# Three-operation float64 conversion through PSUM, and Newton operations one step later, in the first mixture layer

## The chip, the cores and the metric

The kernel runs on one core of a Trainium2 chip. A core has TensorE (PE in the rows; its weight loads are PEld), VectorE (DVE), ScalarE (ACT), GpSimd (POOL) and SyncE (SP, which issues DMAs). The engines run their own instruction streams in order and wait for one another by semaphores. The metric is device time in microseconds (us), from one launch to its end.

## The reference

Three layers follow one another. The first is attention over 4 batches and 8 heads of 512 local and 32 global positions (2304 tokens after the transpose, 512 features). The second, called the first mixture layer here, is a dense layer with a rational activation:

```
h = x @ w_in                                   # 2304x512 @ 512x2048, w_in is float64
P = a[0] + a[1]*h + a[2]*h*h + a[3]*h*h*h
Q = 1 + |b[0]|*|h| + |b[1]|*h*h
x = ((P / (Q + 1e-6)) @ w_out).astype(float32)  # w_out is float64 too
```

The third is a layer of eight experts, each token sent to one. Only the first mixture layer and the conversion of its weights are changed.

## The kernel before

**Weights.** `w_in` and `w_out` come in as float64, as pairs of 32-bit words (low, high). They are worked on in 16 pieces f of 128 hidden units, each with two halves (`w_in`, `w_out`), so there are 32 half pieces of 128x512 elements. `conv` (L881) turns one half into float32. ScalarE takes the magnitude of the high word (L886). VectorE shifts and masks the high word (L887, L888); after a `yield`, so in a later step of the pipeline, it adds bits of the low word (L890) and multiplies with a test for tiny values (L891). The intermediate `st_x` lies in SBUF. `wsplit` (L906) then splits the float32 into two parts, high (ScalarE, L913) and the rest (POOL, L914), since TensorE multiplies in a short format and three products (high x high, high x low, low x high) stand for one.

**Steps.** The layer is cut into 80 steps n = (group g of four pieces f) x (5 blocks of tokens: 512, 512, 384, 384, 384) x (4 pieces). So a group has 20 steps: 8 of 512 tokens and 12 of 384. Steps 0 to 3 are computed within the tail of the attention; the loop of `moe1` runs from step 4 (PRE). In step n:

- `gemm1(n)` (L933): 12 matmuls of 512 or 384 columns into a PSUM bank `h`.
- `poly` (L939 to L942): ScalarE writes `u`, `v`, `t` from `h`; POOL adds `u` and `v` (this is Q - 1).
- `split` of step n-1 (L970 ScalarE, L971 POOL): the finished quotient `t` into `gh` and `gl`.
- `gemm2(n-3)` (L1005 to L1007): 3 matmuls of 512 columns for each 128 tokens, into PSUM banks `o` that gather over the four pieces of a group.
- `poly2` (L947, L948 on VectorE): the polynomial in `t`.
- `inv` (L954, L955 on ScalarE): a first estimate of 1/Q by logarithm and exponential, written over `h`.
- `evac`: where a block's fourth piece is done, VectorE and ScalarE take its `o` banks out (L1013, L1017, L1020; POOL adds for some, L1018).
- `wstep`: one half of a conversion, in most steps.
- `inv2` (L960 to L962 on VectorE): a Newton step on the estimate and the product, `t` being the result.

**What sets the order.** Instructions are issued in the order in which the Python code names them, and each engine keeps it. PSUM has eight banks: four for `o` and two each of the kinds `s` and `t`. From step 4 to step 59 (NSHARE = 60) `hbank` gives `h` all four of `s` and `t` in turn; from step 60 on only the two of `s`, and `t` serves other tiles. `u`, `v` and `t` in SBUF have two buffers each. In the attention a hand-written list of letters (`A_ORDER`) sets the order of each unit's parts; its letter C is one `wstep`.

Of the kernel before, what the change touches and what calls it, by code (L numbers as in the profile page):

```python
# [7 lines left out]
F32 = mybir.dt.float32  # L8
F32R = mybir.dt.float32r
I32 = mybir.dt.int32  # L10
U32 = mybir.dt.uint32
I64 = mybir.dt.int64
AF = mybir.ActivationFunctionType
ALU = mybir.AluOpType
# [5 lines left out]
P = 128  # L20
B, H, SL, SG, D = 4, 8, 512, 32, 64
# [50 lines left out]
PRE = 4  # L72
BLOCKS = [(0, 512), (512, 512), (1024, 384), (1408, 384), (1792, 384)]

NSHARE = 60
KS = [(g, blk, f) for g, grp in enumerate(GROUPS) for blk in BLOCKS for f in grp]


# [4 lines left out]
class Kernel:  # L83
# [5 lines left out]
    def build(self):  # L89
        tc, nc = self.tc, self.nc  # L90
        with ExitStack() as ctx:
# [4 lines left out]
            with tc.manual_schedule(), ExitStack() as pctx, ExitStack() as xctx:  # L96
                self.consts()
                self.xp = ctx.enter_context(tc.tile_pool(name="xp", bufs=1))
                self.xt_hi, self.xt_lo = ([
                    [self.xtile(x, p, c, [P, n], F32R) for p, n in enumerate((HT, NT - HT))] for c in range(NDC)  # L100
                ] for x in ("hi", "lo"))
                self.wr = [[self.xp.tile([P, 2, 4 * CH], F32R, name="wr00")]]
                stage = xctx.enter_context(tc.tile_pool(name="stage", bufs=1, side="right"))
                self.st_raw = [stage.tile([P, CH], F32, name=f"st_raw{i}") for i in range(2)]
                self.st_m = [stage.tile([P, DM], F32, name=f"st_m{i}") for i in range(4)]
                self.st_x = stage.tile([P, DM], U32, name="st_x")
                self.tail = xctx.enter_context(tc.tile_pool(name="tail", bufs=1, side="right"))
                self.mfree, self.mbusy = list(self.st_m), False
                self.w, self.wm, self.wraw, self.G = {}, [], {}, {}
                self.wconv = self.conv()  # L110
                self.ps = pctx.enter_context(tc.tile_pool(name="ps", bufs=1, space=PSUM))
                self.turn, self.oht, self.stg = {}, None, [None] * NCH
                bctx = pctx.enter_context(ExitStack())
                self.wk = bctx.enter_context(tc.tile_pool(name="wk", bufs=2))
                with ExitStack() as actx:
                    self.attention(actx)
                ring = [self.wr[0][0].rearrange("p a b -> p (a b)"), self.tail.tile([P, 4 * CH], F32R, tag="t", name="wslot")]
                self.slot = [ring[i // 4][:, i % 4 * 4 * DM:(i % 4 + 1) * 4 * DM] for i in range(NWR)]
                self.moe1(bctx, ctx, xctx)
                bctx.close()  # L120
                self.moe2_alloc(ctx)
                self.first_hi(range(4, NCH))
                self.route()
# [392 lines left out]
    def attention(self, ctx):  # L516
# [15 lines left out]
        st = {}  # L532
# [4 lines left out]
        def load(u):  # L537
            b, hp = units[u]
            h0 = 2 * hp
            if hp == 0:  # L540
# [1 line left out]
                nc.sync.dma_start(g[0:SG], io["q_g"][b].rearrange("h s d -> s h d"))  # L542
                nc.sync.dma_start(g[SG:], io["k_g"][b].rearrange("h s d -> s h d"))
                st["g", b] = g
            q = self.wk.tile([P, 4, 2, D], F32, tag="t", name="q")
            k = self.wk.tile([P, 4, 2, D], F32, tag="u", name="k")
            for t, src in ((k, "k_l"), (q, "q_l")):
                for h in range(2):
# [327 lines left out]
        self.wraw[f, half] = st  # L876

    def conv(self):
        nc = self.nc
        for f in range(NFC):  # L880
            for half in range(2):  # L881
                st = self.wraw.pop((f, half))
                lo, hi = st[:, :, 0], st[:, :, 1]
                m, x = self.mfree.pop(0), self.st_x
                self.mbusy = True
                nc.scalar.activation(m, hi.bitcast(F32), AF.Abs)  # L886
                nc.vector.tensor_scalar(x, hi, 0x07FFFFFF, 3, ALU.bitwise_and, ALU.logical_shift_left)  # L887
                nc.vector.scalar_tensor_tensor(x, hi, 0xC0000000, x, ALU.bitwise_and, ALU.bitwise_or)  # L888
                yield
                nc.vector.scalar_tensor_tensor(x, lo, 29, x, ALU.logical_shift_right, ALU.bitwise_or)  # L890
                nc.vector.scalar_tensor_tensor(m, m, 2.0 ** -15, x.bitcast(F32), ALU.is_ge, ALU.mult)  # L891
                self.wm.append((f, half, m))
                self.mbusy = False
                if f + 1 < NFC:
# [22 lines left out]
    def hbank(self, k):  # L917

        i = KS.index(k)
        return "st"[i % 2] if PRE <= i < NSHARE else "s"  # L920

    def gemm1(self, k):
        nc = self.nc
        g, (t0, n), f = k
        wh, wl = self.w[f, 0]
        h = self.bank(self.hbank(k), "h")[:, :n]
        self.G[k] = [h] + [self.wk.tile([P, 512], F32, tag=nm, name=nm)[:, :n] for nm in "tuv"]
        i = 0
        for c in range(NDC):
            cs = slice(c * P, (c + 1) * P)  # L930
# [53 lines left out]
    def moe1(self, ctx, kctx, xctx):  # L984
# [111 lines left out]
        while len(pend) > LAG:  # L1096
            gemm2(pend.pop(0))
        for n in range(PRE, NK):
            if n == NSHARE:
                self.lp = self.bank("t", "lp")  # L1100
            while (ks[n][2], 0) not in self.w or n >= LAG and (ks[n - LAG][2], 1) not in self.w:
                self.wstep(freed if n >= LAG else (-2, -2))
# [5 lines left out]
                parts.append((full[0], logits(full.pop())))  # L1108
            elif fin:
                final(fin.pop(0))  # L1110
            if n > 0:
                self.split(ks[n - 1])
            pend.append(ks[n])
            while len(pend) > LAG:
                gemm2(pend.pop(0))
            for x in now:
                logits2(*x)
            self.poly2(ks[n])
            self.inv(ks[n])
            for d in done:  # L1120
                evac(*d)
            done.clear()
            if side and fin:
                final(fin.pop(0))
            norm()
# [12 lines left out]
            g, blk, f = ks[n - LAG + 1]  # L1138
            if f != GROUPS[g][-1] or blk == BLOCKS[0]:
                self.wstep(freed if n >= LAG else (-2, -2))  # L1140
            self.inv2(ks[n])
        n = NK
        bl = len(BLOCKS) - 1
        final(fin.pop(0))
# [572 lines left out]
```

## Time and profile before

| | us |
|---|---|
| median of three runs (926.14 to 930.65) | 928.39 |
| profiled execution | 927.5 |
| its span in the trace | 925.6 |
| busy PE / DVE / ACT / POOL, whole span | 845.2 / 666.2 / 541.8 / 427.2 |

The attention takes the first 187 us or so, the loop of the first mixture layer stands between 208.7 and about 606 us, and the expert layer follows. Busy shares over the whole span mix these stages. PE's ends are modelled, so that PE counts as busy a little longer than it works: its pace is read from the starts of its matmuls.

### The profile page before, as it was taken

The page shows a single profiled execution, that of the slowest core. Times are in us where ns is not written, and L with a number is a line of the kernel's source. Part 1 is how long each engine was busy: PE and PEld are TensorE (multiplying, and loading weights), DVE is VectorE, ACT ScalarE, POOL GpSimd, SP SyncE. Part 2 cuts the span into 40 slices and gives each one's busy share as a digit, 9 for nine tenths or more (in the row PEclk, how much of TensorE's full clock was granted, in tenths as well). Part 3 has the DMA queues.
Part 4 walks back from the last instruction along what each step waited for, and adds up shares of the span by engine and source line. Part 5 has one row for each costly group of instructions (what it writes and reads, how often), then busy time and mean ns, then how long its engine had stood idle before and what let it go on. Part 6 is the DMA issues. An engine that isn't in the chain of part 4 may idle for free.

```text
span 925.6 us, 17451 instructions
## 1 busy us (share of the span) xinstructions
PE 845.2 (91%) x6015; PEld 714.0 (77%) x6015; DVE 666.2 (72%) x1320; ACT 541.8 (59%) x1180; POOL 427.2 (46%) x381
## 2 busy tenths in 40 slices
PE   7888999879999999999998999977899999999994
PEld 5566777668887878777786888856779889898983
DVE  3786888888998999999998777788726793222620
ACT  5665676557778877777777787764434551113211
POOL 4333333445556676666756543314615781112400
PEclk9997999999999999999999999989899999999998
DMA  7555555201111101111010024236924884111000
GB/s 168 126 135 134 122 129 133 69 23 47 46 46 46 46 24 46 47 46 46 27 44 0 2 77 139 75 131 210 319 80 145 288 313 145 36 35 60 28 25 15
DMA packets 106501, 84.96 MB, mean 92 GB/s; under 512 B 79175, under 2 KB 87367, under 8 KB 106384
## 3 DMA queue, kind: packets, MB, share of 16 engines
q1 hardware_dynamic: 102864, 73.18, 26.8%
q0 software_dynamic: 3520, 10.23, 3.2%
q8 instruction: 72, 1.18, 0.5%
q14 instruction: 45, 0.37, 0.1%
HBM read 74.47 MB, written 10.22 MB: 91 GB/s over the span
## 4 chain that ended last, share of the span: by engine, by line
PE 49%; DVE 32%; issue 7%; ACT 5%; DMA 3%; SPq 2%; POOL 1%; DVEq 0%; ACTq 0%; POOLq 0%
PE d_o L1421 13%; PE d_h L1381 10%; PE h L933 5%; DVE t L948 4%; DVE t L962 4%; DVE h L961 4%; DVE u L960 4%; DVE t L947 4%; PE sb L646 3%; PE d_h L1395 3%; DVE st_x L890 3%; DVE st_x L887 1%; DMA q<-q_l 1%; PE o L1005 1%; PE o L1007 1%
## 5 line engine op out<-in xcount | busy, mean ns | idle before, releaser
L933 PE MATMUL h<-xhi,wr 128*128 128x384 f32 (+1 forms) x480 | 146.2, 365 | 8.0 <-DVE t L962 8.0
L942 POOL TENSOR_TENSOR u<-u,v 128x384 f32<-128x384 f32 (+1 forms) x80 | 92.2, 1153 | 90.3 <-ACT v L940 79.3
L1421 PE MATMUL d_o<-wr,xlo 128*128 (+1 forms) x528 | 127.1, 399 | 7.1 <-DVE wr L1548 3.9
L1421 PEld LDWEIGHTS d_o<-wr,xlo 128*128 128x128 f32 x528 | 99.9, 192 | 29.9 <-issue 6.1
L971 POOL TENSOR_TENSOR gl<-t,gh 128x384 fp32r<-128x384 f32 (+1 forms) x80 | 92.1, 1151 | 63.0 <-issue 36.0
L933 PEld LDWEIGHTS h<-xhi,wr 128*128 128x128 f32 x480 | 90.2, 191 | 18.3 <-DVE t L962 9.0
L1381 PEld LDWEIGHTS d_h<-xlo,wr 128*128 128x128 f32 x768 | 94.6, 195 | 2.9 <-issue 2.3
L1381 PE MATMUL d_h<-xlo,wr 128*128 128x256 f32 x768 | 95.0, 286 | 1.9 <-issue 1.9
L1005 PE MATMUL o<-wr,gh 128*128 128x512 f32 x204 | 82.7, 405 | 8.4 <-DVE x L1020 4.7
L933 PE MATMUL h<-xlo,wr 128*128 128x384 f32 (+1 forms) x240 | 86.8, 362 | 0.0
L1489 ACT ACTIVATE xlo<-d_h 128x512 fp32r<-128x512 f32 x32 | 19.0, 597 | 106.7 <-PE d_h L1381 106.7
L1007 PE MATMUL o<-wr,gl 128*128 128x512 f32 x204 | 80.5, 394 | 0.0
L1006 PE MATMUL o<-wr,gh 128*128 128x512 f32 x204 | 80.4, 394 | 0.0
L970 ACT CAST gh<-t 128x384 fp32r<-128x384 f32 (+1 forms) x80 | 44.9, 561 | 54.3 <-DVE t L962 53.4
L1653 POOL TENSOR_TENSOR wr<-xhi,wr 128x1024 f32 x21 | 61.8, 2956 | 28.1 <-ACT wr L1478 18.5
L1548 DVE TENSOR_TENSOR wr<-xhi,wr 128x1024 f32 x35 | 68.6, 2008 | 3.8 <-issue 3.6
L1639 POOL DMA_INDIRECT out<-xlo,scat x22 | 25.2, 1146 | 89.7 <-DVE xlo L1581 88.4
L1581 DVE TENSOR_SCALAR xlo<-d_o,gate 128x512 f32<-128x512 f32 x22 | 16.4, 748 | 66.2 <-PE d_o L1421 66.2
L960 DVE SCALAR_TENSOR_TENSOR u<-u,h 128x384 f32<-128x384 f32 (+1 forms) x80 | 48.2, 602 | 18.7 <-ACT h L955 13.6
L673 ACT ACTIVATE pr<-pr,nm 128x160 f32<-128x160 f32 x128 | 53.0, 425 | 14.6 <-DVE rs L683 10.5
L687 POOL TENSOR_TENSOR pr<-pr,rs 128x512 f32<-128x512 f32 x32 | 38.8, 1232 | 46.6 <-DVE rs L684 39.6
L941 ACT ACTIVATE t<-h,ab 128x384 f32<-128x384 f32 (+1 forms) x80 | 57.5, 718 | 0.7 <-POOL gl L971 0.7
(288 smaller groups left out, 2069.7 us busy)
## 6 DMA issues: line engine op xcount, KB each, us to landing
xhi<-w SPq DMA_DIRECT2D x64, 512.0 KB, 5.1
st_raw<-w_in SPq DMA_DIRECT2D x16, 512.0 KB, 3.8
st_raw<-w_out SPq DMA_DIRECT2D x16, 512.0 KB, 3.7
x_dram<-x SPq DMA_DIRECT2D x17, 256.0 KB, 2.2
k<-k_l SPq DMA_DIRECT2D x32, 128.0 KB, 3.5
q<-q_l SPq DMA_DIRECT2D x32, 128.0 KB, 3.7
va<-v_l SPq DMA_DIRECT2D x32, 96.0 KB, 2.7
vb<-v_l SPq DMA_DIRECT2D x32, 96.0 KB, 2.7
```

Source lines behind the costliest of these rows:

```text
L933: nc.tensor.matmul(h, w[:, cs], x, start=(i == 0), stop=(i == 3 * NDC - 1))
L941: nc.scalar.activation(t, h, AF.Identity, bias=self.ab[:, 2:3], scale=self.ab[:, 3:4])
L942: nc.gpsimd.tensor_tensor(u, u, v, ALU.add)
L960: nc.vector.scalar_tensor_tensor(u, u, ONE, h, ALU.add, ALU.mult)
L971: nc.gpsimd.tensor_tensor(gl, t, f32(gh), ALU.subtract)
L1005: nc.tensor.matmul(o, gh[:, gs], wh[:, DM:], start=first, stop=False)
L1006: nc.tensor.matmul(o, gh[:, gs], wl[:, DM:], start=False, stop=False)
L1007: nc.tensor.matmul(o, gl[:, gs], wh[:, DM:], start=False, stop=last)
L1381: r = nc.tensor.matmul(o, w(0, par, b, sl), xs[a][:, c], start=(i == 0), stop=(i == len(steps) - 1))
L1421: r = nc.tensor.matmul(po[t], ht[a][h][:, c, t * P:(t + 1) * P], w(1, par, b, sl), start=(h == c == a == b == 0), stop=(h == a == 1 and c ...
L1548: E.tensor_tensor(l_, stg[i], f32(h_), ALU.subtract).then_inc(ld, 1)
L1653: E.tensor_tensor(l_, stg[i], f32(h_), ALU.subtract).then_inc(lp, 1)
```

## The change

1. `conv`: ScalarE copies the high word scaled by 2^-112 into `m` (it took the magnitude before); VectorE's two bit operations read `m` and no longer the raw high word; the last operation writes `m` and the multiplication goes. So VectorE has three operations for a half instead of four, and its first one waits for ScalarE's copy.
2. From step 4 to step 65 the intermediate is a PSUM bank `xb` of the kind `t`, not `st_x`. In the attention it stays `st_x`.
3. `h` then has three banks in turn (`sts`) in place of four, up to step 65 (NSHARE = 66).
4. Up to step 65 `inv2` of step n-1 follows `inv` of step n, and `split` of step n-2 stands where that of n-1 was. `t` has three buffers; `u` and `v` still have two.
5. `evac` of a block's first two tiles stands ahead of `poly2`, the rest behind it and ahead of `inv`.

```diff
-NSHARE = 60
+NSHARE = 66
-            q = self.wk.tile([P, 4, 2, D], F32, tag="t", name="q")
+            q = self.wk.tile([P, 4, 2, D], F32, tag="t", name="q", bufs=3)
...
-                m, x = self.mfree.pop(0), self.st_x
+                m, x = self.mfree.pop(0), self.st_x if self.xb is None else self.xb
-                nc.scalar.activation(m, hi.bitcast(F32), AF.Abs)
-                nc.vector.tensor_scalar(x, hi, 0x07FFFFFF, 3, ALU.bitwise_and, ALU.logical_shift_left)
-                nc.vector.scalar_tensor_tensor(x, hi, 0xC0000000, x, ALU.bitwise_and, ALU.bitwise_or)
+                y = m.bitcast(U32)
+                nc.scalar.activation(m, hi.bitcast(F32), AF.Copy, scale=2.0 ** -112)
+                nc.vector.tensor_scalar(x, y, 0x0FFFFFFF, 3, ALU.bitwise_and, ALU.logical_shift_left)
+                nc.vector.scalar_tensor_tensor(x, y, 0x80000000, x, ALU.bitwise_and, ALU.bitwise_or)
                 yield
-                nc.vector.scalar_tensor_tensor(x, lo, 29, x, ALU.logical_shift_right, ALU.bitwise_or)
-                nc.vector.scalar_tensor_tensor(m, m, 2.0 ** -15, x.bitcast(F32), ALU.is_ge, ALU.mult)
+                nc.vector.scalar_tensor_tensor(y, lo, 29, x, ALU.logical_shift_right, ALU.bitwise_or)
...
-        return "st"[i % 2] if PRE <= i < NSHARE else "s"
+        return "sts"[i % 3] if PRE <= i < NSHARE else "s"
...
+            if n == PRE:
+                self.xb = self.bank("t", "xb").bitcast(U32)
             if n == NSHARE:
+                self.xb = None
...
-            if n > 0:
+            behind = n < NSHARE
+            if n == NSHARE:
+                self.inv2(ks[n - 1])
+                self.split(ks[n - 2])
+            if behind and n > PRE:
+                self.split(ks[n - 2])
+            elif not behind:
                 self.split(ks[n - 1])
...
+            for d in done[:2]:
+                evac(*d)
             self.poly2(ks[n])
+            for d in done[2:]:
+                evac(*d)
             self.inv(ks[n])
-            for d in done:
-                evac(*d)
             done.clear()
+            if behind and n > PRE:
+                self.inv2(ks[n - 1])
...
-            self.inv2(ks[n])
+            if not behind:
+                self.inv2(ks[n])
```

On VectorE, steps 22 and the start of 23 stood like this before (`h_4031` is the bank of step 22, `h_4079` that of 23, `o` the gathered banks that go out):

```order
L947 TENSOR_TENSOR t_4032<-t_4032,h_4031 128x512
L948 SCALAR_TENSOR_TENSOR t_4032<-t_4032,ab_209,h_4031 128x512
L1013 COPY x2_14_3186<-o_3922 128x512
L1013 COPY x2_16_3187<-o_3930 128x512
L887 TENSOR_SCALAR st_x_98<-st_raw0_92 128x512
L888 SCALAR_TENSOR_TENSOR st_x_98<-st_raw0_92,st_x_98 128x512
L960 SCALAR_TENSOR_TENSOR u_4033<-u_4033,h_4031 128x512
L961 SCALAR_TENSOR_TENSOR h_4031<-u_4033,h_4031 128x512
L962 SCALAR_TENSOR_TENSOR t_4032<-t_4032,ab_209,h_4031 128x512
L947 TENSOR_TENSOR t_4080<-t_4080,h_4079 128x512
L948 SCALAR_TENSOR_TENSOR t_4080<-t_4080,ab_209,h_4079 128x512
```

The same steps on VectorE now (`h_3969` is the bank of step 21, `h_4009` of 22, `h_4057` of 23):

```order
L1022 COPY x2_14_3177<-o_3901 128x512
L956 TENSOR_TENSOR t_4010<-t_4010,h_4009 128x512
L957 SCALAR_TENSOR_TENSOR t_4010<-t_4010,ab_209,h_4009 128x512
L1022 COPY x2_16_3178<-o_3909 128x512
L969 SCALAR_TENSOR_TENSOR u_3971<-u_3971,h_3969 128x512
L970 SCALAR_TENSOR_TENSOR h_3969<-u_3971,h_3969 128x512
L971 SCALAR_TENSOR_TENSOR t_3970<-t_3970,ab_209,h_3969 128x512
L897 TENSOR_SCALAR xb_3198<-st_m0_94 128x512
L898 SCALAR_TENSOR_TENSOR xb_3198<-st_m0_94,xb_3198 128x512
L956 TENSOR_TENSOR t_4058<-t_4058,h_4057 128x512
L957 SCALAR_TENSOR_TENSOR t_4058<-t_4058,ab_209,h_4057 128x512
```

One copy out of `o` moved ahead of the polynomial, the three Newton operations are those of the step before, and the conversion reads `st_m` and writes `xb`. On ScalarE, from the exponential of step 22 to that of step 23, with the engines that an instruction waits for, it was before:

```order
L955 ACTIVATE h_4031<-v_4034 128x512 [waits DVE_49,Activation_49]
L1013 COPY x2_14_3186<-o_3926 128x512 [waits PE_49]
L913 CAST wr00_88<-st_m3_97 128x512
L886 ACTIVATE st_m0_94<-st_raw0_92 128x512 [waits DMAHW4_49]
L939 ACTIVATE u_4081<-h_4079,ab_209 128x512 [waits PE_49]
L940 ACTIVATE v_4082<-h_4079,sb1_211 128x512
L941 ACTIVATE t_4080<-h_4079,ab_209 128x512 [waits Pool_49]
L970 CAST gh_4099<-t_4032 128x512 [waits DVE_49]
L954 ACTIVATE v_4082<-u_4081,one_265 128x512 [waits Pool_49]
L955 ACTIVATE h_4079<-v_4082 128x512 [waits DVE_49,Activation_49]
```

And it is now:

```order
L964 ACTIVATE h_4009<-v_4012 128x512 [waits DVE_49,Activation_49]
L922 CAST wr00_88<-st_m3_97 128x512
L896 ACTIVATE st_m0_94<-st_raw0_92 128x512 [waits DMAHW4_49]
L948 ACTIVATE u_4059<-h_4057,ab_209 128x512 [waits DVE_49,PE_49]
L949 ACTIVATE v_4060<-h_4057,sb1_211 128x512
L950 ACTIVATE t_4058<-h_4057,ab_209 128x512 [waits Pool_49]
L979 CAST gh_4077<-t_3970 128x512 [waits DVE_49]
L963 ACTIVATE v_4060<-u_4059,one_265 128x512 [waits Pool_49]
L964 ACTIVATE h_4057<-v_4060 128x512 [waits DVE_49,Activation_49]
```

The copy out of `o` went ahead of the logarithm, `gh` is made of the `t` of step 21 and no longer of 22, and the first instruction of a step, which writes `u`, has a wait for VectorE that it did not have.

## Rows read from the trace of the kernel before

**Rows 1.** Windows, steps 4-19, 20-39, 40-59: us, PE, PEld, DVE, ACT, POOL, clock, DMA.
```profile
208.70:286.00 77.30, 74.88 (x359) 65.04 (x358) 70.00 (x110) 60.58 (x113) 42.04 (x37) 1.00 0.13 42
286.00:386.50 100.50, 96.40 (x446) 82.24 (x445) 94.18 (x140) 78.66 (x144) 66.79 (x54) 0.98 0.13 42
386.50:489.30 102.80, 96.86 (x446) 82.22 (x445) 96.99 (x142) 79.12 (x145) 70.21 (x57) 0.98 0.13 42
```

**Rows 2.** Waits of PE from 205 to 525 us: total, times, longest.
```profile
PE o L1005 <- DVE x L1020: 8.8, 5, 2.3
PE h L933 <- DVE t L962: 2.6, 1, 2.6
```

**Rows 3.** Timeline of PE: first matmul of steps 4, 37, 38, 64 and 65 (start, us).
```profile
208.70 0.39 PE L933 MATMUL h<-xhi,wr 128*128 128x512 f32 x1
...
371.88 0.34 PE L933 MATMUL h<-xhi,wslot 128*128 128x384 f32 x1
...
376.04 0.33 PE L933 MATMUL h<-xhi,wr 128*128 128x384 f32 x1
...
513.37 0.39 PE L933 MATMUL h<-xhi,wr 128*128 128x512 f32 x1
...
518.80 0.39 PE L933 MATMUL h<-xhi,wr 128*128 128x512 f32 x1
```

**Rows 4.** Groups by line and form, DVE, 205 to 525 us: busy, mean ns | idle.
```profile
L890 DVE SCALAR_TENSOR_TENSOR st_x<-st_raw,st_x 128x512 uint32<-128x512 uint32 x24 | 24.3, 1011 | 0.0
L888 DVE SCALAR_TENSOR_TENSOR st_x<-st_raw,st_x 128x512 uint32<-128x512 uint32 x23 | 23.1, 1002 | 0.8
L891 DVE SCALAR_TENSOR_TENSOR st_m<-st_m,st_x 128x512 f32<-128x512 f32 x24 | 22.7, 945 | 0.8
...
L887 DVE TENSOR_SCALAR st_x<-st_raw 128x512 uint32<-128x512 uint32 x23 | 18.9, 820 | 0.0
...
L961 DVE SCALAR_TENSOR_TENSOR h<-u,h 128x512 f32<-128x512 f32 x26 | 18.1, 696 | 0.9
```

**Rows 5.** Lines L888 and L961, 205 to 525 us: ns minimum/median/maximum, first and last start.
```profile
L888 DVE SCALAR_TENSOR_TENSOR st_x<-st_raw,st_x x23: 691/694/1764, 217.2 to 493.9; 128x512 uint32<-128x512 uint32 x23
...
L961 DVE SCALAR_TENSOR_TENSOR h<-u,h x62: 561/563/697, 210.2 to 521.3; 128x384 f32<-128x384 f32 x36, 128x512 f32<-128x512 f32 x26
```

**Rows 6.** Timeline of DVE: Newton of step 37, polynomial of step 38.
```profile
381.40 0.56 DVE L960 SCALAR_TENSOR_TENSOR u<-u,h 128x384 f32<-128x384 f32 x1 [0.70 <-ACT h L955]
381.99 0.56 DVE L961 SCALAR_TENSOR_TENSOR h<-u,h 128x384 f32<-128x384 f32 x1
...
383.12 0.55 DVE L947 TENSOR_TENSOR t<-t,h 128x384 f32<-128x384 f32 x1
383.70 0.61 DVE L948 SCALAR_TENSOR_TENSOR t<-t,ab,h 128x384 f32<-128x384 f32 x1
```

**Rows 7.** Timeline of ACT: a step with conversion, and the one after it.
```profile
376.80 0.61 ACT L913 CAST wslot<-st_m 128x512 fp32r<-128x512 f32 x1
377.31 0.67 ACT L886 ACTIVATE st_m<-st_raw 128x512 f32<-128x512 f32 x1
...
380.80 0.50 ACT L955 ACTIVATE h<-v 128x384 f32<-128x384 f32 x1
381.23 0.57 ACT L939 ACTIVATE u<-h,ab 128x384 f32<-128x384 f32 x1
381.69 0.57 ACT L940 ACTIVATE v<-h,sb 128x384 f32<-128x384 f32 x1
382.16 0.67 ACT L941 ACTIVATE t<-h,ab 128x384 f32<-128x384 f32 x1
```

**Rows 8.** Chain that ended last, one conversion in the attention (start, us).
```profile
124.24 1.41 DVE st_m L891
```

**Rows 9.** Timeline of PE behind that conversion.
```profile
125.16 0.65 PE L705 MATMUL tb<-ident,pr 128*128 128x128 f32 x4 [0.35 <-POOL pr L687]
126.31 0.44 PE L709 MATMUL tb<-ident,pgl 128*128 128x128 f32 x2 [0.50 <-DVE pt L581]
```

## Prediction before the run

> **What bounds the kernel now.** I read the windows first, then PE's waits, then the starts of PE's matmuls, and after that the groups and timelines of the two engines that PE waits for.
>
> In the windows the reader is to see that steps 4 to 59 have two engines near their limit: in the two full groups of 20 steps VectorE is busy 94.2 of 100.5 us and 97.0 of 102.8, with PE at 96.4 and 96.9 [rows 1]. PE's figure is flattered by modelled ends, so I take its own pace from starts. Between steps 64 and 65 it does 24 matmuls of 512 columns in 518.80 - 513.37 = 5.43 us, 0.226 each; between steps 37 and 38 twelve of 384 and nine of 512 in 4.16 us, so the twelve cost 4.16 - 9 x 0.226 = 2.12 [rows 3]. gemm1 of a step goes with gemm2 of three steps earlier, so a group has 3 steps of 512 with three tiles (21 x 0.226 = 4.75), 5 of 512 with four (5.43), 3 of 384 with four (2.12 + 12 x 0.226 = 4.84) and 9 of 384 with three (4.16): 14.3 + 27.2 + 14.5 + 37.4 = 93.4 us. The groups took 100.5 and 102.8 [rows 1].
>
> Steps 4 to 63 took 513.37 - 208.70 = 304.7 us [rows 3]. At PE's pace they take 4 x 5.43 + 14.5 + 37.4 = 73.6 for steps 4 to 19, 2 x 93.4, and 3 x 4.75 + 5.43 = 19.7 for steps 60 to 63: 280.1. So 24.6 us are lost there, and that is all this stage can give. Of it 8.8 is listed as waits of gemm2 for VectorE to take `o` out, 2.6 as a wait of gemm1 for a bank of `h` after the Newton step [rows 2]; much of the rest is PE at its lower clock behind such waits (mean clock 0.98 in both groups, which contain stretches at 1.2 GHz) [rows 1]. So PE is late because VectorE is late.
>
> **The conversion.** VectorE's four operations take 0.82 + 1.00 + 1.01 + 0.95 = 3.78 us for a half [rows 4]. L888 goes from 0.69 at its minimum and median to 1.76 [rows 5]; the operations that have one operand in PSUM do not spread: L961, 62 times, never above 0.70 [rows 5]. Both have the same 512 elements at most and stand among the same POOL work. So I price the three new operations by L961 at 512 columns, 0.70 [rows 4]: 2.1 us, a saving of 1.7. Bounds: 0.56 each (L961 at 384 columns, fewer elements) gives a saving of 2.1; 1.76 each (L888's maximum, if the bank shields nothing) gives a loss of 1.5. A group has 8 halves: VectorE gets 13.4 us back, between +17 and -12. Its busy time becomes about 81 and 84 us, below PE's 93.4.
>
> The Trainium skill ("VectorE: DVE Perf Modes", section "Why PSUM operands drop a tier") speaks against the bank here: an fp32 operation with any PSUM operand has only one element per cycle, while a one-source operation within SBUF has two. By its cycle table the first operation would go from about (58 + 256) / 0.96 = 0.33 us to (120 + 512) / 0.96 = 0.66, an estimate. In this kernel L887 averages 0.82 anyhow [rows 4], so the loss of the faster mode costs nothing against the mean; had all four run at their quickest (0.33 + 3 x 0.69 = 2.40), it would leave a saving of only 0.3 per half, 2.4 us per group.
>
> VectorE's first operation now waits for ScalarE's copy. Behind it the second one and the next polynomial are queued. ScalarE reaches the end of the copy after the exponential, the split and the copy, about 0.43 + 0.51 + 0.67 = 1.6 us after the exponential starts [rows 7]; VectorE fills that with three Newton operations, some 1.7 (0.59 start to start [rows 6], three times). It is covered, barely; uncovered it costs the difference, a few tenths.
>
> **The later Newton step makes a new ring.** `u` still has two buffers, so ScalarE's first operation of a step now waits for the second Newton operation of two steps earlier, which VectorE does behind the polynomial of the step before. The ring per step of 384: L948 0.61, L960 0.59, L961 0.56 [rows 6], then ScalarE's three 0.46 + 0.47 + 0.67 [rows 7], then L947 to L948 0.58 [rows 6]: 3.94, and two wake-ups of 0.10 (L960 started at 381.40, the exponential that it waited for ended at 381.30 [rows 6, 7]): 4.14. PE's step is 4.16 or 4.84. In a step that starts a conversion the way leads by the exponential and two copies instead: 0.61 + 0.10 + 0.43 + 0.51 + 0.67 + 0.46 + 0.47 + 0.67 + 0.10 + 0.58 = 4.60. With three such steps in eight: 4.3; with a copy out of `o` (0.70, priced as L961) in one step of four, about 4.45. At 512 columns each of the seven operations takes 0.13 more (0.696 against 0.563 [rows 4, 5]): 5.05, or 5.5 with a conversion, 5.25 on average. A group by the ring: 8 x 5.25 + 12 x 4.45 = 95.4, that is 4.77 per step, against PE's 93.4 and the 100.5 to 102.8 of now. So the ring is what is late next, by about 2 us per group, 2.4 with what the other engines add: I keep 7 us lost over the three groups' worth of steps and count 24.6 - 7 = 17.5 us as gained. Bounds: ring hidden, 24.6; ring 0.25 dearer per step (each of its wake-ups 0.2 instead of 0.1 and a little from POOL), 60 x 0.25 = 15 less, 2.5.
>
> The three banks for `h` belong to it: gemm1(n) needs the third Newton operation of step n-3, done in step n-2. From the end of gemm1(n-2) that is 1.6 (ScalarE) + 0.1 + 1.2 (polynomial) + 1.7 = 4.6 us, and PE fills 2.04 + 2.12 + 2.04 = 6.2 before it needs the bank: 1.6 to spare, 1.0 where a copy out stands between.
>
> The copies out of `o` ahead of `poly2` cost nothing by themselves: the tiles are complete 0.7 us (three matmuls) into gemm2, while the polynomial waits some 1.7 for ScalarE. They attack the 8.8 us.
>
> **Attention.** Eight conversions end there, each with L891 at 1.41 us, six of these in the chain that ended last (one of them: [rows 8]). Behind it PE waited 0.50 for VectorE's copy [rows 9]. With L891 gone the copy can start 1.4 earlier, but PE's transposes before it wait for POOL until 125.16 and end at 125.81 [rows 9], so 0.50 of it can come out: 6 x 0.5 = 3 us. Bounds: 6 x 1.41 = 8.5, and below nothing, -5, since the first operation waits for ScalarE's copy (0.67 [rows 7]) eight times. I take 3. The third buffer of `q`, and the order from step 66 on, I cost at nothing: PE's instructions stay as they were.
>
> **Sum.** 927.5 - 17.5 - 3 = 907.0 us against the profiled execution, which lies 0.9 below the median of 928.39.
>
> **Rivals.**
> - *The ring hides* (chance 0.13): PE's pace alone, 927.5 - 24.6 - 3 to 5 = 895 to 901. For it: starts on one engine are closer than durations. Against it: the conversion steps' 4.60.
> - *The waits for `o` stay* (0.18): they are PE's own, since four banks must turn round within one gemm1, and the 8.8, with the lower clock behind them, some 12, remain: about 917. Against it: the second group of tiles has 2 us more than it needs when VectorE is on time.
> - *The ring is dearer by 0.25* (0.08): 4.77 + 0.25 = 5.0 per step, nearly what it is now: 921 to 926.
> - *Slower, the bank shields nothing* (0.05): conversion operations in PSUM wait for POOL as L888 at its worst, VectorE gets 12 us per group more, 106 to 109, and PE follows it: three groups' worth, 927.5 + 20 - 3 = 944. It decides from a mean of 1.26 per operation (3 x 1.26 = 3.78). L961's maximum of 0.697 speaks against it [rows 5].
>
> **How the numbers follow.** The forecast, 901 to 913, has 0.56. The range reaches from 898 into the second rival, 919, and leaves out less than 0.2. Faster by over 0.5% (below 923.8, about what a measurement can tell) sums to 0.89: forecast, first and second rival, and part of the third. Within 0.5%: 0.06. Slower: 0.05.
>
> **What would show it.** L897, L898, L900 at 0.7 with no tail to 1.7; VectorE busy 80 to 85 us per group, groups 95 to 97 long by the starts of PE's gemm1; ScalarE's first operation of a step waiting for L970; no long wait of gemm2 for L1029; in the attention the transposes of `pgl` waiting for POOL's chain instead of the copy. It is wrong if the new operations average over 1.0, if PE waits for L971 at many steps, or if the groups stay at 100.

## The result and the profile after

The changed kernel takes 903.15 us, the median of four runs (896.24 to 906.70), against 928.93 for the kernel before in the same comparison: ratio 0.9715, 95% interval 0.968 to 0.9751. The forecast was 907.0 with a range of 898 to 919. The profiled execution is the shortest of the four, 896.24 us with a span of 894.3, so its total flatters the change and its stages are compared one by one. A second set of runs of the same kernel on another chip gave 901.51 against 927.66, ratio 0.9721 [0.9681, 0.9762].

The page: busy time of each engine, and the chain that ended last, by engine and by line.

```profile
PE 835.5 (93%) x6015; PEld 711.2 (80%) x6015; DVE 621.3 (69%) x1288; ACT 542.1 (61%) x1180; POOL 412.4 (46%) x381
...
PE 81%; DVE 5%; issue 4%; SPq 3%; DMA 3%; POOL 1%; ACT 1%; DVEq 0%; POOLq 0%; ACTq 0%
```

Before, PE held 49% of that chain and VectorE 32%. Now PE holds 81%. Line numbers from L881 on are higher by 9 or 10: gemm1 is L942, ScalarE's first operation L948, the polynomial L956 and L957, Newton L969 to L971, gemm2 L1014 to L1016.

First matmuls of steps 4 and 64 in PE's timeline (start, us):

```profile
202.62 0.39 PE L942 MATMUL h<-xhi,wr 128*128 128x512 f32 x1
...
484.90 0.39 PE L942 MATMUL h<-xhi,wr 128*128 128x512 f32 x1
```

Windows of steps 20 to 39 and 40 to 59 (us, PE, PEld, DVE, ACT, POOL, granted clock, DMA share, GB/s), which answer to the last two lines of [rows 1]:

```profile
276.70:370.80 94.10, 94.10 (x445) 81.44 (x444) 82.53 (x133) 79.67 (x145) 63.28 (x55) 1.00 0.14 45
370.80:465.00 94.20, 94.20 (x445) 81.46 (x444) 82.55 (x133) 79.53 (x146) 65.00 (x57) 1.00 0.14 45
```

The reader is to see that PE is busy for the whole of each window, at a granted clock of 1.00, and VectorE has dropped from 94.2 and 97.0 [rows 1] to 82.5. Waits between 202 and 490 us, steps 4 to 64 (total, times, longest); PE, which had 8.8 and 2.6 us in [rows 2], waits for nothing in that stretch:

```profile
DVE t L956 <- ACT t L950: 24.3, 42, 1.9
...
ACT u L948 <- DVE h L970: 11.4, 21, 0.7
...
DVE xb L897 <- ACT st_m L896: 2.6, 3, 1.8
```

The conversion, L897, L898 and L900, from step 4 on (ns minimum/median/maximum); [rows 5] is the counterpart:

```profile
L897 DVE TENSOR_SCALAR xb<-st_m x23: 685/689/695, 211.4 to 468.4; 128x512 uint32<-128x512 uint32 x23
...
L898 DVE SCALAR_TENSOR_TENSOR xb<-st_m,xb x23: 695/695/697, 212.1 to 469.1; 128x512 uint32<-128x512 uint32 x23
...
L900 DVE SCALAR_TENSOR_TENSOR st_m<-st_raw,xb x23: 679/680/681, 216.8 to 473.3; 128x512 uint32<-128x512 uint32 x23
```

69 operations, none above 0.697 us.

**Where the 31.3 us between the two profiled executions lie.** All stretches are counted between first matmuls of steps. Steps 4 to 63 took 484.90 - 202.62 = 282.3 us instead of 304.7: 22.4. Step 4 starts 208.70 - 202.62 = 6.1 earlier. From step 64 to step 79 it took 80.8 instead of 82.6: 1.8. What follows took 328.6 instead of 329.7: 1.1.

Part of the 6.1 is chance. Before step 4, PE ran at 1.2 GHz in these stretches (windows of the kernel before, same columns):

```profile
19.80:23.20 3.40, 3.40 (x22) 2.08 (x21) 2.28 (x14) 2.42 (x7) 2.38 (x3) 0.51 1.22 292
81.20:91.40 10.20, 9.17 (x82) 6.99 (x78) 3.37 (x18) 3.01 (x10) 2.52 (x3) 0.50 0.80 185
193.80:197.20 3.40, 3.32 (x8) 2.64 (x9) 3.33 (x6) 1.90 (x4) 3.12 (x2) 0.50 0.00 0
```

That is 17.0 us at half the clock, against three stretches of 3.4 in the changed kernel. Counting half of such a stretch as lost, which is an estimate, 8.5 - 5.1 = 3.4 of the 6.1 are clock and 2.7 are the attention's own. The lengths of these stretches differ from run to run of one kernel: the second set's profiled run of the changed kernel had 6.8 us of them, started step 4 at 201.5, and took the same 282.27 for the loop. So below the loop is compared directly, and the start of step 4 after taking off half of its 1.2 GHz stretches. Corrected in this way, step 4 starts at 199.4 to 201.9 us in the four kernels with four operations in the attention (before, c, k, l) and at 195.6 to 199.5 in the ten profiled runs with three, 2.9 earlier on average.

### The profile page after: what moved, and what is told of

Its sections match the earlier page's. It is cut to its first block, busy times and chain, and to the rows that moved or that the text cites. A ratio compares the mean times of both kernels' runs of the same rounds, so it can differ in the third digit from the quotient of the medians.

```text
span 894.3 us, 17479 instructions
## 1 busy us (share of the span) xinstructions
PE 835.5 (93%) x6015; PEld 711.2 (80%) x6015; DVE 621.3 (69%) x1288; ACT 542.1 (61%) x1180; POOL 412.4 (46%) x381
## 4 chain that ended last, share of the span: by engine, by line
PE 81%; DVE 5%; issue 4%; SPq 3%; DMA 3%; POOL 1%; ACT 1%; DVEq 0%; POOLq 0%; ACTq 0%
PE h L942 21%; PE d_o L1444 14%; PE d_h L1404 10%; PE o L1014 7%; PE o L1016 7%; PE o L1015 7%; PE d_h L1418 4%; PE sb L649 3%; DMA q<-q_l 2%; PE gob L820 1%; SPq L552 1%; PE d_x L1373 1%; PE tb L708 1%; PE lb L761 1%; PE xb L729 1%
## 5 line engine op out<-in xcount | busy, mean ns | idle before, releaser
L942 PE MATMUL h<-xhi,wr 128*128 128x384 f32 (+1 forms) x480 | 145.0, 363 | 3.2 <-DVE t L971 3.2
L951 POOL TENSOR_TENSOR u<-u,v 128x384 f32<-128x384 f32 (+1 forms) x80 | 90.4, 1130 | 123.9 <-ACT v L949 97.5
L942 PEld LDWEIGHTS h<-xhi,wr 128*128 128x128 f32 x480 | 89.5, 189 | 12.7 <-DVE t L971 3.6
L942 PE MATMUL h<-xlo,wr 128*128 128x384 f32 (+1 forms) x240 | 86.5, 360 | 0.0
L1014 PE MATMUL o<-wr,gh 128*128 128x512 f32 x204 | 81.2, 398 | 0.0
L1016 PE MATMUL o<-wr,gl 128*128 128x512 f32 x204 | 80.0, 392 | 0.0
L1015 PE MATMUL o<-wr,gh 128*128 128x512 f32 x204 | 79.8, 391 | 0.0
L1571 DVE TENSOR_TENSOR wr<-xhi,wr 128x1024 f32 x35 | 72.8, 2126 | 3.8 <-issue 3.6
L948 ACT ACTIVATE u<-h,ab 128x384 f32<-128x384 f32 (+1 forms) x80 | 49.7, 621 | 32.7 <-PE h L942 18.4
L956 DVE TENSOR_TENSOR t<-t,h 128x384 f32<-128x384 f32 (+1 forms) x80 | 48.5, 606 | 29.3 <-ACT t L950 28.3
L963 ACT ACTIVATE v<-u,one 128x384 f32<-128x384 f32 (+1 forms) x80 | 53.4, 668 | 12.4 <-POOL u L951 12.0
```

Of the source, the lines that this page charges most:

```text
L942: nc.tensor.matmul(h, w[:, cs], x, start=(i == 0), stop=(i == 3 * NDC - 1))
L951: nc.gpsimd.tensor_tensor(u, u, v, ALU.add)
L963: nc.scalar.activation(v, u, AF.Ln, bias=self.one)
L1014: nc.tensor.matmul(o, gh[:, gs], wh[:, DM:], start=first, stop=False)
L1015: nc.tensor.matmul(o, gh[:, gs], wl[:, DM:], start=False, stop=False)
L1016: nc.tensor.matmul(o, gl[:, gs], wh[:, DM:], start=False, stop=last)
```

## Experiments

Theories at the start. The prediction's: VectorE's load set the pace; three short operations free it, the later Newton step covers the wait for ScalarE's copy, and the ring over `u` becomes the next limit. First rival: the bank alone does it (the operations become short because one operand is in PSUM, however many there are). Second rival: the order alone does it (later Newton, early copies out). The main kernels in a table; "loop" is from the first matmul of step 4 to that of step 64 in the profiled run, "group" steps 20 to 39, "64-79" from the first matmul of step 64 to that of step 79, all in us. The kernels ran on three chips; each ratio is to the kernel before on the same chip.

| | conversion: operations, place | Newton | copies out of o | loop | group | 64-79 | median | ratio to before |
|---|---|---|---|---|---|---|---|---|
| before | 4, SBUF | own step | late | 304.7 | 100.5 | 82.6 | 926.9 to 928.9 | 1 |
| a | 3, SBUF | own step | late | 329.2 | 111.9 | 82.6 | 949.56 | 1.0243 [1.0192, 1.0294] |
| k | 4, PSUM | own step | late | 283.6 | 94.1 | 82.6 | 906.42 | 0.9762 [0.9726, 0.9797] |
| b | 3, PSUM | own step | late | 304.4 | 100.7 | 82.6 | 924.45 | 0.9966 [0.9938, 0.9994] |
| f | 3, PSUM | own step | early | 300.4 | 100.5 | 80.8 | 916.22 | 0.9890 [0.9853, 0.9927] |
| c | 4, SBUF | later | early | 306.0 | 101.8 | 80.9 | 925.62 | 0.9976 [0.9949, 1.0004] |
| d | 3, SBUF | later | early | 288.2 | 95.8 | 80.8 | 907.93 | 0.9778 [0.9734, 0.9822] |
| e | 3, PSUM | later | late | 286.8 | 95.3 | 83.5 | 906.64 | 0.9775 [0.9732, 0.9817] |
| l | 4, PSUM | later | early | 282.3 | 94.2 | 80.8 | 902.08 | 0.9712 [0.9673, 0.9750] |
| o | 4, PSUM; 3 in the attention | own step | early | 282.3 | 94.2 | 80.8 | 900.47 | 0.9706 [0.9661, 0.9750] |
| after | 3, PSUM | later | early | 282.3 | 94.2 | 80.8 | 903.15 | 0.9715 [0.9680, 0.9751] |

### a: the three operations alone

```diff
-                nc.scalar.activation(m, hi.bitcast(F32), AF.Abs)
+                nc.scalar.activation(m, hi.bitcast(F32), AF.Copy, scale=2.0 ** -112)
...
-                nc.vector.scalar_tensor_tensor(m, m, 2.0 ** -15, x.bitcast(F32), ALU.is_ge, ALU.mult)
```

The kernel before with change 1 only; the intermediate stays in SBUF.

> The kernel before with the three-operation conversion alone; its intermediate stays in SBUF, four banks for h, Newton step and copies out of o where they were. Theory (VectorE's load was the bound, and what POOL does to it counts): a half costs 0.8 + 1.0 + 1.0 = 2.8 us in place of 3.8, VectorE gets 8 us per group back, groups of 96 to 98 in place of 100.5 to 102.8, the attention gives 3: 912 to 916 us. Rival (the order of the steps made the loss, not the load): the loop stays at 304 us and only the attention gains: 924 to 926.

Measured: 949.56, 2.4% slower than before with one VectorE operation fewer; both forecasts had it faster. The waits, 205 to 525 us:

```profile
DVE st_x L888 <- ACT st_m L887: 39.2, 23, 2.8
...
PE o L1005 <- DVE x L1020: 18.3, 6, 4.9
```

The same kernel's VectorE groups (busy, mean ns | idle before):

```profile
L889 DVE SCALAR_TENSOR_TENSOR st_x<-st_m,st_x 128x512 uint32<-128x512 uint32 x23 | 25.7, 1118 | 0.8
L891 DVE SCALAR_TENSOR_TENSOR st_m<-st_raw,st_x 128x512 uint32<-128x512 uint32 x24 | 25.6, 1068 | 0.0
L888 DVE TENSOR_SCALAR st_x<-st_m 128x512 uint32<-128x512 uint32 x23 | 23.6, 1027 | 39.2 <-ACT st_m L887 39.2
```

The operation that goes saves 23 x 0.95 = 22 us [rows 4], but the three that are left take 3.21 us per half instead of the 2.83 of L887, L888 and L890 [rows 4], and VectorE stands 1.7 us in front of each first one. The copies out of `o`, queued behind, come late, and PE's waits for them double against [rows 2]. Part of the loss is clock: from step 4 to step 64 PE spent 30.7 us at 1.2 GHz (mean granted clock 0.95), before 10.2 (0.98). Half of the difference, 10 of the 24.5 us by which the loop is longer, is estimated to be that.

### k: the bank alone

```diff
-                m, x = self.mfree.pop(0), self.st_x
+                m, x = self.mfree.pop(0), self.st_x if self.xb is None else self.xb
...
-        return "st"[i % 2] if PRE <= i < NSHARE else "s"
+        return "sts"[i % 3] if PRE <= i < NSHARE else "s"
```

The kernel before with all four operations, through the PSUM bank (and so three banks for `h`, NSHARE = 66). Like all kernels here that are made from the changed one, it also has the third buffer of `t`. That cannot be what pays: before, ScalarE waited for a buffer of `t` once in the loop, for 0.7 us.

> The kernel before with its four-operation conversion, whose intermediate goes through PSUM in the loop (three banks for h, up to step 65); Newton step and copies as before. Its first operations read the raw words, so there is no wait for ScalarE's copy. Theory (load and waits of VectorE are what counts): four operations at 0.70 take 2.8 in place of 3.8, 8 us per group less, and no new wait: groups of 96 to 99, 912 to 919. Rival (three banks or the old order hold the loop where it was): 924 or more.

Measured: 906.42, better than the 912 to 919 expected; the loop falls to 283.6, which is 21.1 of the change's 22.4 us. Its four VectorE operations (ns minimum/median/maximum):

```profile
L896 DVE TENSOR_SCALAR xb<-st_raw x23: 682/686/689, 215.5 to 474.5; 128x512 uint32<-128x512 uint32 x23
...
L897 DVE SCALAR_TENSOR_TENSOR xb<-st_raw,xb x23: 695/696/698, 216.3 to 475.2; 128x512 uint32<-128x512 uint32 x23
...
L899 DVE SCALAR_TENSOR_TENSOR xb<-st_raw,xb x23: 684/689/690, 221.1 to 480.1; 128x512 uint32<-128x512 uint32 x23
...
L900 DVE SCALAR_TENSOR_TENSOR st_m<-st_m,xb x23: 686/686/691, 221.8 to 480.8; 128x512 f32<-128x512 f32 x23
```

Its windows of steps 20 to 39 and 40 to 59:

```profile
283.10:377.24 94.14, 94.14 (x445) 81.47 (x444) 86.58 (x141) 79.16 (x144) 62.71 (x54) 1.00 0.14 45
377.24:472.00 94.76, 94.67 (x446) 81.31 (x444) 86.63 (x142) 79.18 (x145) 65.22 (x57) 1.00 0.15 45
```

Four operations take 2.76 us per half, 1.02 less than in SBUF (3.78 [rows 4]), with the number of operations unchanged. VectorE's 86.6 us per group are below PE's 94.1, and that is enough: PE waits for nothing from step 4 to step 64.

The Trainium skill ("SBUF — State Buffer", section "Who interferes with whom") says that VectorE's operations with two SBUF inputs contend with a GpSimd instruction that reads SBUF, that those in a two-port mode contend with GpSimd too, and that those with at most one SBUF input, outside such a mode, do not. The trace agrees: L888 with both inputs in SBUF spreads from 0.69 to 1.76 [rows 5], and the same operation here, with one of them in PSUM, stays between 0.695 and 0.698. The first operation has a single input; before, within SBUF, it went from 0.415 to 1.345, here from 0.682 to 0.689:

```profile
L887 DVE TENSOR_SCALAR st_x<-st_raw x23: 415/948/1345, 216.4 to 492.9; 128x512 uint32<-128x512 uint32 x23
```

### b and f: three operations through the bank, Newton in its own step

```diff
-            behind = n < NSHARE
+            behind = False
```

The changed kernel without the later Newton step; in b the copies out of `o` are late again too, in f they stay early.

> The changed kernel with its Newton operations and its copies out of o put back where they were before: the conversion has three operations and goes through PSUM, h has three banks. Theory: VectorE is at 81 to 84 us per group, so that it is on time for the copies out of o; nearly all of the loop's 22 us come back: 904 to 908. Rival (the waits of gemm2 for o are PE's own and need the copies ahead of the polynomial): some 9 to 12 us of the loss stay: 913 to 917.

> The changed kernel with the Newton operations in their own step; the conversion has three operations through PSUM, the copies out of o stand early. Theory: VectorE's first conversion operation waits some 1.6 us for ScalarE's copy, as in the run without the later Newton step (38.0 us in 23 waits); the early copies out of o take away PE's waits of 9.5 us but not that one: groups of 98 to 101, 914 to 922. Rival (the early copies do it): 908 or below.

Measured: 924.45, outside both forecasts for b, and 916.22, as f's theory had it. The wait for ScalarE's copy in b, with a wait of PE:

```profile
DVE xb L897 <- ACT st_m L896: 38.0, 23, 2.6
...
PE o L1014 <- DVE x L1029: 9.5, 6, 2.4
```

and in f:

```profile
DVE xb L897 <- ACT st_m L896: 35.3, 23, 1.9
...
PE o L1014 <- DVE x L1029: 6.1, 6, 1.8
```

The early copies were expected to take away PE's 9.5 us; 6.1 are left.

Steps 20 to 39 in the windows of f:

```profile
279.09:379.55 100.46, 96.07 (x446) 80.87 (x444) 81.86 (x133) 78.61 (x145) 62.09 (x54) 1.00 0.13 42
```

VectorE is busy only 81.9 of 100.5 us in f and the group is as long as before. So the load is not all: 35.3 / 23 = 1.5 us at the head of each conversion hold up the three Newton operations that stand behind it, and what follows them. Against k, which has one operation more and no such wait, b loses 304.4 - 283.6 = 20.8 us. The wait takes back all that the bank gave.

### c and d: the new order without the bank

```diff
-                m, x = self.mfree.pop(0), self.st_x if self.xb is None else self.xb
+                m, x = self.mfree.pop(0), self.st_x
```

d is the changed kernel with the intermediate in SBUF; c also has the old four operations. In both, the bank kept for `xb` is then free for `h`.

> The changed kernel with the old four-operation conversion in SBUF: only the order is new (Newton step later, copies out of o early); the bank that xb held goes to h in turn. Theory: VectorE still needs 94 to 97 us per group, more than PE's 93.4, but idles less: groups of 96 to 99, 915 to 922. Rival (the order did it): 905 or below.

> The changed kernel with the intermediate of the conversion in SBUF; the bank that xb held goes to h in turn. Theory: single operations of the conversion go up to 1.7 us again where POOL works, VectorE is at 87 to 90 per group; the mean is under PE's 93.4, so a loss of 1 to 4 us against the changed kernel: 904 to 908. Rival 1 (the shielding decides, since the ring of VectorE and ScalarE has no slack): 910 or more. Rival 2 (only the number of operations counts): equal to the changed kernel within 0.3%.

Measured: 925.62, outside both forecasts for c, and 907.93, within d's 904 to 908. Steps 20 to 39 of c, and what PE waits for between 205 and 525 us:

```profile
287.13:388.95 101.82, 97.85 (x445) 80.22 (x444) 96.65 (x142) 79.36 (x146) 70.67 (x55) 1.00 0.13 42
...
PE o L1016 <- POOL gl L980: 10.6, 22, 0.8
```

Steps 20 to 39 of d:

```profile
281.31:377.08 95.77, 95.50 (x446) 80.85 (x444) 86.55 (x134) 79.32 (x146) 67.11 (x55) 1.00 0.14 45
```

The conversion's groups in d (busy, mean ns | idle before), beside those of a:

```profile
L898 DVE SCALAR_TENSOR_TENSOR st_x<-st_m,st_x 128x512 uint32<-128x512 uint32 x23 | 24.0, 1044 | 0.8
L900 DVE SCALAR_TENSOR_TENSOR st_m<-st_raw,st_x 128x512 uint32<-128x512 uint32 x24 | 19.5, 812 | 0.0
L897 DVE TENSOR_SCALAR st_x<-st_m 128x512 uint32<-128x512 uint32 x23 | 19.0, 826 | 3.0 <-ACT st_m L896 2.7
```

In c VectorE is as full as before, and the order gives nothing: PE's waits for `o` to be taken out are gone, but PE now waits for the low part `gl` of the split instead. In d three operations in SBUF, with the wait for the copy covered by the later Newton step, bring VectorE to 86.6, the load of k, and 16.5 of the 22.4 us. So there are two ways to relieve VectorE, the bank or three operations with the later Newton step (d has the early copies too). Together they do not add up, because PE's pace of 94.2 per group is reached.

### e: the copies out of o late

```diff
-            for d in done[:2]:
-                evac(*d)
             self.poly2(ks[n])
-            for d in done[2:]:
-                evac(*d)
             self.inv(ks[n])
+            for d in done:
+                evac(*d)
```

> The changed kernel with the copies out of o behind the polynomial and the exponential, as before. Theory (conversion and Newton step do it together, the early copies are a small part): VectorE is on time, PE waits for o for 0 to 4 us in the loop: 903 to 908. Rival (the early copies carry a good part, since the four banks of o must turn round within one gemm1): 910 to 916.

Measured: 906.64, within the theory's 903 to 908, with 1.2 us listed as waits of PE in the loop; loop 286.8 (4.5 more than the changed kernel) and steps 64 to 79 83.5 (2.7 more). So the early copies are worth 7.2 us in the profiled runs here, 5.8 between b and f (4.0 and 1.8), and 3.1 between k and o (1.3 and 1.8).

### l, m and o: which part of the three operations is needed

l is the changed kernel with four operations, m the kernel before with three operations in the attention's nine halves alone, o is k with m's three operations in the attention and the early copies.

```diff
+                if 2 * f + half < 9:
+                    y = m.bitcast(U32)
+                    nc.scalar.activation(m, hi.bitcast(F32), AF.Copy, scale=2.0 ** -112)
...
+                else:
+                    nc.scalar.activation(m, hi.bitcast(F32), AF.Abs)
```

> The changed kernel with the old four operations through PSUM: new order, shielded, one operation more for a half. Theory: VectorE is at 86 to 89 us per group, under PE's 93.4, and the ring of VectorE and ScalarE has some slack: the loop stays at PE's pace within 2 us, the attention loses 2 to 3: 905 to 909. Rival (the third operation less is needed for the loop): groups of 96 and more, 911 or above.

> The kernel before, with the three-operation conversion for the first nine halves alone, which are those of the attention (in SBUF); the loop keeps its four operations in SBUF and its order. Theory (each of the eight conversions at the end of the attention gives back what L891 held up there, and ScalarE's copy costs VectorE nothing there): step 4 starts about 2.8 us earlier, the loop stays at 304 to 306 us, 924 us, ratio 0.997. Rival A (the 2.8 us that the three-operation kernels showed come from where the loop's first conversions stand, not from the attention): step 4 starts where it did, 926 to 928, ratio 1.000. Rival B (VectorE's wait for the copy costs in the attention what it costs in the loop, 1.6 us a conversion): step 4 starts 5 us or more later, 930 or more.

> The kernel before with the PSUM intermediate and three banks for h, the four-operation conversion in the loop, the three-operation one for the nine halves of the attention, the Newton operations in their own step (as before), and the first two copies out of o ahead of the polynomial. It thus has what the runs so far paid for and not the later Newton step. Theory (the bank gives 21 us of the loop, three operations give 2.8 in the attention, the early copies 1.8 in steps 64 to 79): loop 282 to 284, steps 64 to 79 80.8, 901 to 904, ratio 0.971 to 0.974, the same as the change itself. Rival (the later Newton step is needed as well): loop 286 or more, 906 or more, ratio 0.977 or more.

Measured: l 902.08 (905 to 909 expected), m 923.73 against 927.66 (ratio 0.9964 [0.9932, 0.9996]; 924 expected), o 900.47 (901 to 904 expected). In l and o the loop is 282.3, as in the changed kernel: the fourth operation costs nothing there once the bank is used. m's loop took 302.9, and its step 4 starts here:

```profile
203.06 0.39 PE L941 MATMUL h<-xhi,wr 128*128 128x512 f32 x1
```

That is 5.6 earlier than before [rows 3]; m has 10.2 us at 1.2 GHz ahead of it, before has 17.0, so by the estimate 3.4 of it are clock and 2.2 the conversion's, near the 2.8 expected. One start could be chance; PE's waits in the attention are clearer. They are for the copy that [rows 9] shows, from the launch to step 4. Before:

```profile
PE tb L709 <- DVE pt L581: 3.8, 8, 0.5
```

in m:

```profile
PE tb L709 <- DVE pt L581: 0.5, 1, 0.5
```

and in the changed kernel:

```profile
PE tb L712 <- DVE pt L584: 0.3, 1, 0.3
```

In every run with four operations in the attention (before, c, k, l) there are seven places behind a conversion where the first transpose of `pgl` starts 0.76 to 0.77 us after the transpose before it; in every run with three operations it is 0.11 at all seven. So the gain does come from the attention, against rival A, and step 4 starts earlier and not later, against rival B. o, with no later Newton step, stands beside the changed kernel on the same chip at 900.47 to 901.51, with intervals that lie over one another. These runs do not show it to be faster, but they show that the later Newton step is not needed when the conversion keeps its four operations.

### n: the changed kernel once more

> The changed kernel once more, unaltered, so that it stands beside the other kernels on the same chip: 900 to 905, ratio 0.971, loop 282.3, no wait of PE in steps 4 to 63. If a chip's own spread made the earlier difference, it lies elsewhere by more than 3 us.

Measured: 901.51 (894.28 to 903.25), ratio 0.9721, loop 282.27, no wait of PE in steps 4 to 63, as expected.

### i: how long is the ring?

```diff
             nc.scalar.activation(u, h, AF.Abs, scale=self.ab[:, 4:5])
+        if PRE <= KS.index(k) < NSHARE:
+            nc.scalar.activation(u, h, AF.Abs, scale=self.ab[:, 4:5])
```

> The changed kernel with ScalarE's first operation of a step (the magnitude that writes u) issued twice in steps 4 to 65: the ring over the two buffers of u becomes longer by one ScalarE operation, 0.46 at 384 columns and 0.59 at 512, 10 us for a group of 20 steps; ScalarE has 90 of 94 us to do, still less than PE. By the prediction's price of the ring (95.4 per group): 104 to 105 per group, loop 312 to 315, 933 to 936. By the ring priced from starts and not from durations (some 91 per group): 100 to 101, loop 300 to 303, 921 to 924. If the ring is no limit at all here (under 84 per group): 94 to 95, loop 282 to 285, 903 to 906. The wait of ScalarE's L948 for VectorE's L972 tells how far the ring is the limit.

Measured: 932.46, ratio 1.0062 [1.0033, 1.009]; both full groups 104.5, loop 312.5. One turn of the ring in the chain (start, us, what):

```profile
306.61 0.70 ACT u L949
307.34 0.69 ACT u L950
308.03 0.57 ACT v L951
308.60 0.68 ACT t L952
309.31 0.70 DVE t L958
310.03 0.75 DVE t L959
310.78 0.61 DVE u L971
311.41 0.71 DVE h L972
312.15 0.04 issue
312.20 0.70 ACT u L949
```

The window of steps 20 to 39:

```profile
278.00:382.50 104.50, 99.80 (x446) 79.66 (x445) 82.32 (x134) 91.80 (x164) 61.39 (x53) 1.00 0.13 41
```

The groups fell where the prediction's price of the ring had put them (104 to 105; the total of 932.46 lies just below its 933 to 936), but for a wrong reason, and the rows say so. The chain between 278 and 487 us names no line of PE among its larger shares: the group is the ring's. A plain turn at 512 columns takes 312.20 - 306.61 = 5.59, and the added operation in it not the 0.59 I had counted but 307.34 - 306.61 = 0.73 (0.716 on average, and 0.611 at 384 columns). Over a group that is 12 x 0.611 + 8 x 0.716 = 13.1, so the ring without it comes to 104.5 - 13.1 = 91.4. That is the second theory's 91, and 2.8 below PE's 94.2.

The chain cuts overlapping pieces short. The starts of instructions at two places of that turn, from the timeline:

```profile
308.50 0.78 ACT L952 ACTIVATE t<-h,ab 128x512 f32<-128x512 f32 x1
...
309.31 0.69 DVE L958 TENSOR_TENSOR t<-t,h 128x512 f32<-128x512 f32 x1 [0.67 <-ACT t L952]
...
310.03 0.75 DVE L959 SCALAR_TENSOR_TENSOR t<-t,ab,h 128x512 f32<-128x512 f32 x1
...
310.69 0.68 DVE L971 SCALAR_TENSOR_TENSOR u<-u,h 128x512 f32<-128x512 f32 x1
```

## Why the prediction was right, point by point

- **What bounds the kernel.** Right: PE was late because VectorE was; k and d, which relieve VectorE in different ways, both bring the loop near PE's pace. PE's own pace was priced a little too short: 93.4 per group and 280.1 for steps 4 to 63, against 94.2 and 282.3 where PE does not wait at all. So 22.4 us were to be had, not 24.6. The lower clock had less to do with it than I said ("much of the rest"): three stretches of 3.4 us lie in those steps, half of which is 5.1. Three more waits of PE for `o`, 1.3, 1.3 and 1.1 us, were left out of the prediction's account; with them the listed waits come to 15.1.
- **The conversion.** Right in size: 0.69 + 0.695 + 0.68 = 2.07 per half for 2.1, VectorE 82.5 per group for "81 and 84". The pricing by L961, the operation with one operand in PSUM, held to 0.02 us. The estimates for the first operation, 0.33 us at its quickest in SBUF and 0.66 with the bank (by a form that reads PSUM, while this one writes it), measure 0.415 and 0.69. What the step did not see is which part of it pays in the loop: the bank's 1.02 us per half already frees enough, and the removal of L891 adds nothing there (l and after have the same loop).
- **The wait for ScalarE's copy.** "Covered, barely" is right: 2.6 us in 3 waits. "Uncovered it costs the difference, a few tenths" is wrong in size: 1.5 to 1.7 us each, in b, f and a, and in b it took back some 20 us of the loop. With the bank, the later Newton step only covers the wait that the removed operation brings in; o has neither in the loop and is as quick.
- **The ring.** The mis-sized term. The prediction had 95.4 per group, late by 2, and kept 7 us lost on account of it. It comes to 91.4, and PE never waits for it, so 22.4 came out instead of 17.5. The ring is there, as the prediction's signs said: ScalarE's first operation waits for L970 21 times, 11.4 us in all; it only stays hidden behind PE. A plain turn at 512 columns without the added operation is 5.59 - 0.73 = 4.86 for the 5.05 priced. Most pieces had been priced from start to start, but two were durations that are too long: the polynomial's second operation, 0.74 priced, takes 310.69 - 310.03 = 0.66 to the start of the next, and ScalarE's last operation with its wake-up, 0.90 priced, takes 309.31 - 308.50 = 0.81. These two are 0.17 of the 0.19. How much of the 4.0 per group lies in the turns with a conversion or a copy was not taken apart. The rival "the ring hides" (0.13) was the truth for the loop, with the floor of 282.3 in place of 280.1.
- **Waits for o.** The rival that they stay (0.18) is out: no wait of PE is left. The early copies do what the prediction hoped: without them (e) the loop is 4.5 longer.
- **Attention.** Right, in place and size: 3 predicted; 2.7 in the changed kernel and 2.2 in m after the clock is taken off, and PE's waits for the copy fall from 3.8 us to 0.3 and 0.5.
- **Costed at nothing.** Steps 64 to 79 gain 1.8. They do so in each kernel of the table with the early copies (80.8 to 80.9) and in none with the late ones (82.6 to 83.5), so it is the copies that pay there, and not the three operations. This was missing from the sum. The order from step 66 on and the third buffer of `q` cost nothing that shows.
- **Slower, the bank shields nothing** (0.05): excluded by the 69 operations below 0.70.

The forecast of 907.0 is 3.9 us above the median of 903.15. The sum had a ring that cost 7 us too much and a floor of the loop that was 2.2 too low; that these partly cancel is luck, and together they make 4.9 (22.4 - 17.5). Steps 64 to 79 add 1.8. With these two terms put right the sum is 907.0 - 4.9 - 1.8 = 900.3, inside the changed kernel's 896.24 to 906.70. The 2.9 us from there to the median are not traced to anything; over the four runs the mean granted clock goes from 0.979 in the shortest to 0.968 in the longest.

## What to carry to other kernels

Look at the spread of an operation, not its mean: one that takes 0.69 at its minimum and 1.76 at its maximum is held up by somebody, and moving one of its operands to PSUM can be worth more than removing an operation (k against a). Before an instruction is taken away from a full engine, ask what the new first instruction waits for: three operations behind a ScalarE copy were slower (a) than four that wait for nothing. Price a ring from start to start, not from durations, and measure it by lengthening it by one known operation whose own length is read in the same run.

## What the runs showed of the hardware that was not expected

- Left in SBUF, the same VectorE operation becomes slower when its neighbours move: the first of the three took 1.03 on average in a and 0.83 in d, the third 1.07 and 0.81, though nothing in them differs. They are slow where they meet POOL's work: of the 328 conversion operations in the loops of before, a, c and d, 60 overlap no instruction of POOL, and none of these takes more than 0.694 us; those that overlap one average 0.90 to 1.29 us, line by line.
- The interference goes both ways. With the conversion in SBUF and the new order POOL is busy 70.7 us in a group with four operations (c) and 67.1 with three (d); with it in PSUM 63.3 (after), with the same POOL instructions. POOL's spans in a profile are rough, but these are like against like.
